# One more unit's w_out product by seven half-size products, its sums shared with VectorE, and the instruction list made anew

## The chip, the cores and the metric

The kernel runs on one core of a Trainium2 chip. Its engines are TensorE (PE, matrix products; PEld is its weight load), VectorE (DVE), ScalarE (ACT), GpSimd (POOL) and SyncE (SP, which issues the loads and stores); each works through a list of its own in order. The metric is the device time of one execution in microseconds (us).

## The reference

Packed attention, and a SwiGLU layer on its result, in fp32:

```python
p_packed = sm_attn(p, k, v)           # (8 batches, 8 heads, 32, 64), keys 576
out = sm_attn(q, p_packed, p_packed)  # (8, 8, 576, 64)
x = out.transpose(0, 2, 1, 3).reshape(4608, 512)
xn = x / sqrt(mean(x * x) + 1e-6) * rms_g
g, val = xn @ w_gate, xn @ w_val      # 512 to 1536
return (g * sigmoid(g) * val) @ w_out # 1536 to 512
```

## The kernel before

The 4608 tokens are worked in twelve units u = 0 to 11 of 384 tokens, three tiles of 128 each. For each unit the attention of its tokens comes first (the keys, the packed values and the weights of a batch are made once per batch), then the SwiGLU layer. Each fp16 product on TensorE stands for one of fp32: an operand is a hi and a lo half, and three products (hi by hi, hi by lo, lo by hi) are summed in PSUM.

*First product* (`mlp`, line 1527): for each of 12 slices ft of the 1536 columns, gate and val in a PSUM room each, six matmuls of 384 columns (twelve of 192 where the unit lies over two batches). `gated` takes them to SBUF: ScalarE's Silu (line 1609), VectorE's multiply (line 1612), then the hi half by ScalarE or VectorE and the lo half, a subtract, by GpSimd or VectorE (lines 1634, 1637, 1640), into the tile `hall`.

*Second product*: for one tile of tokens, 36 matmuls of 512 columns (12 slices by three, line 1592) into one PSUM room of four (pm), and a scaled copy to a tile of SBUF and a store (`store`, line 1800). For the units from `STR_FROM` = 6 on, only tile 2 is done so. Tiles 0 and 1 go by Strassen's method in Winograd's form (`seven`, line 1723): the two tiles and pairs of slices (a chunk c, six in all) form a 2 x 2 block matrix, w_out another, and seven products k = 1, 6, 7, 5, 2, 4, 3, each 18 matmuls of 256 columns, take the place of eight. What this needs:

- sums of blocks of the unit's gated tiles: `parts_of`, four adds or subtracts of 128x128 for each chunk (line 1677, by GpSimd or VectorE in turn, `SUM_BY`), cast to hi by ScalarE (line 1686) and to lo by GpSimd (line 1689); the halves of the blocks themselves by lines 1653, 1656 and 1659.
- sums of blocks of w_out, made once: `tees`, for each of six chunks (tee 0 to 5) two adds of 128x512 (line 1132) and four subtracts of 128x256 (line 1135), all by GpSimd (`TEE_BY`), then ScalarE's cast (line 1139) and VectorE's low (line 1141) into `teev`, a region of the tile wgv that is free once batch 3's packed weights are done.
- `together` (line 1738) adds the seven products up on VectorE and stores.

The order of the work is written out. Each part of the kernel is a generator (a chain); `Plan.run` goes through the table `ORDER`, at each entry lets the chain of that number issue its next step, and hands out rooms (PSUM and SBUF buffers) from pools as they are asked for. A step such as ("tee", d) waits until the mark is there. So the table fixes the order on every engine. `FILLS` puts dummy matmuls (line 1826) ahead of certain TensorE steps. Names of rooms in the rows: pm, psa and psb are PSUM; o_0x and o_1x are the two rooms that sums, tees and stores share; t and a are gated tiles.

Of the kernel before, what the change touches and what calls it, by code (L numbers as in the profile page):

```python
# [15 lines left out]
P = 128  # L16
# [28 lines left out]
class Plan:  # L45
# [84 lines left out]
    "ABAAAAAAAAAAADAAAWAEAFAAAAAAAAAAAAAAAAADAAAAAAAAAAAAABAxADAxAyADAxADAEAyAWAWAxAxAxAxAGAHAWAxAyAEAxAEAFAxAFAFAyAW"  # L130
    "AWAWAxAQAyAyAyAyAQAQAyAQAyACAGAyAQAIACAHAGAIAHACAQACAGACAIAJAXACARAHAXAXAIAXARAJACAJARAXAJAKARAKAXASASALAWALAWAX"
    "ARACAQAMAXAXASAKAYASALAKAXAXAXASAYALAXAXAzAXARATAWATAzAWAYATAXAXAMAXAzAMAXAYA0ATAMA0ATANAXANA0AOAPAaAAAAAAAAAzAA"
    "AAASAYANAbAYAUAcATANARAXA2A2AOAUA0AWAXA2AYAWAWAUA2AXAYAPA1AOASA3AOAUA3APAWAZAVAAAUAAAZAUAPA3A7A1AAAAAZAAA7AaAVAA"
    "AAAaA3AZAVAaATA8AAA1AbAAAAAbAYAAAVAaAAAaAbAAAAAZA8AcAcAVAcA8AYA9A9AZA5AdA7AdA8A7A-AdAeA-AdAbAZAZAcA9AZA+A-AeA+A5"
    "A9A-AZAZAZAfAeAcBAA5A+AeAdBAAVAfBAA+A6AfA1AbA6AYA5A4A4A5BAA5A5A5A6BBAeAZAZAeAdA5AfAUA6AfBCBBA1AVA6BCAZA6A6BCAfBB"
    "A6AgAYBBAgAZBEAgBEAZAZBDBDArA5BCBDA1BFA6A5ArA6AsBFBDBEAZACAZA6ACBEArACAsACAtACBGACBGAZAXACBFACAXBGAZAZAZBFAsBGAC"
    "ACBHACBIAWACACAZAXAtAYBHBIACAXAtAAAAAAAAAAAAAvBIAuAWAABHAZAZAZAZAZAZBHAZAZAuAXAWAAAXAAAZAZAXAuAZAvAXAYAXAXAZAWAA"
    "AwAYAZAZAwBJAXAvAABJAABJAXBJAZAZBIAXAwAXAXAWAZAZAZAZAAAXAXAWAXAXAWAWAWAZAZAZAZAZAZAXAWAXAZBKBLAWAAAXAYAAAAAXAABM"
    "AXBMAXAAAZBMAAAXAABMAZAZAZAXAABLBKAZAXAAAZAZAZAZAZAZAXAABNAZBOAZAXAYBOBPBPAYBOAZAXBPBOAABRAXBQBQAXBQAABQBRAZAZAZ"
# [45 lines left out]
    "EKAZAZAZAZEMAZAZAXAZAZAZAZAZAZEMEMEMAZAZELAZAZAZEMEMAZAZAZENEMAZENAZEMAZEMENEOAZAZEMEOEOAZEPAZENEPEQEQEPEOAZEOEO"
    "EQAZEOEOAZEPERESAZEOAZEREQEQEQEQEQEOESAZAZEQEOEOEQEREOETEOERETEQESEUESEQAZAZAZEUETESAZEUESEQESESESEVEVAZEUETEUES"
    "EWEWAZAZAZEUESEVEVEUEUEUEXEUAZEWEXEQEUEUEUEXEWEXAZAZAZEWEWEYEYEUEYEYEYEWESEYAZAZAZEWEYEWEWESEWEYEYEWESAZEYEWEYAZ"
    "AZAZEYAZEYEYAZEWAZAZAZAZAZEaAZAZAZAZAZEaAZEaAZEZEaEZAZAZAZAZAZAZEaEaEaEaAZEaAZEaEa"
# [1693 lines left out]
```

## Time and profile before

| | |
|---|---|
| time, median of 3 runs | 715.92 us (715.59 to 718.26) |
| the profiled execution | 717.6 us, its span 715.8 us, mean granted TensorE clock 0.998 |
| TensorE busy | 697.8 us, 97% of the span |
| VectorE, ScalarE, GpSimd busy | 515.4 us (72%), 496.2 us (69%), 350.1 us (49%) |
| chain that ended last | TensorE 81%, DMA 6%, VectorE 4%, ScalarE 4%, GpSimd 3% |

The span is shorter than the execution's time by what lies around it. A busy share is a mean over the whole span: an engine at 72% can be without a gap in one stretch and half idle in another. The chain is followed back from the last instruction, at each step to what released it. Line numbers are those of the kernel before; in the kernel after, lines from 190 on stand two lower in the file, those from `seven`'s wait on three.

### The profile page before, as it was taken

How to read it: one execution, taken by the hardware profiler on the slowest of the kernel's cores; microseconds unless marked ns; L12 is line 12 of the kernel's file. 1: busy time of each engine (PE TensorE's matmuls, PEld its weight loads, DVE VectorE, ACT ScalarE, POOL GpSimd, SP SyncE). 2: the span in 40 equal slices, each digit the busy share in tenths (PEclk: the TensorE clock that was granted, in tenths of full speed). 3: DMA queues.
4: the chain of work that ended last, by engine and by line, in shares of the span. 5: the costliest groups of instructions: out<-in, count | busy, mean ns of one | idle time of the engine just before them, and what ended most of it. 6: DMA issues, size and time to landing. Idle time of an engine off the chain costs nothing.

```text
span 715.8 us, 20438 instructions
## 1 busy us (share of the span) xinstructions
PE 697.8 (97%) x8367; PEld 460.4 (64%) x8367; DVE 515.4 (72%) x1126; ACT 496.2 (69%) x1095; POOL 350.1 (49%) x468
## 2 busy tenths in 40 slices
PE   8889999999999999989999999999999999999998
PEld 6755655874554564676454555886855766987656
DVE  4788898775976877767879988787666756665342
ACT  3588887886787787578687789588387466473350
POOL 2486632341343364456656459158158076165290
PEclk9999999999999999999999999999999999999999
DMA  9996903677288858964989769787747653421001
GB/s 294 367 375 260 239 3 83 104 164 167 50 166 186 253 136 209 210 115 145 247 225 210 183 113 248 162 224 234 186 138 192 124 164 64 148 104 38 31 0 45
DMA packets 157103, 118.23 MB, mean 165 GB/s; under 512 B 117201, under 2 KB 140497, under 8 KB 153170
## 3 DMA queue, kind: packets, MB, share of 16 engines
q1 hardware_dynamic: 157010, 116.94, 63.5%
q8 instruction: 65, 1.06, 0.6%
q14 instruction: 28, 0.23, 0.1%
HBM read 72.88 MB, written 15.73 MB: 124 GB/s over the span
## 4 chain that ended last, share of the span: by engine, by line
PE 81%; DMA 6%; DVE 4%; ACT 4%; POOL 3%; issue 2%; SPq 1%; POOLq 0%; ACTq 0%; DVEq 0%
PE pm_1x L1527 9%; PE pm_3x L1527 9%; PE pm_0x L1527 8%; PE pm_2x L1527 8%; PE pm_3x L1592 8%; PE pm_2x L1592 7%; PE pm_0x L1592 5%; PE pm_1x L1723 3%; PE pm_0x L1723 3%; PE pm_3x L1723 3%; PE pm_2x L1723 2%; DMA ring<-in_moe_w_gate_dram 2%; PE psa L1086 1%; PE psb L915 1%; PE psa L1327 1%
## 5 line engine op out<-in xcount | busy, mean ns | idle before, releaser
L1527 PEld LDWEIGHTS <-ring 128*128 128x128 f16 x2304 | 204.7, 98 | 86.5 <-issue 14.9
L1592 PEld LDWEIGHTS <-hall 128*128 128x128 f16 x792 | 74.9, 98 | 89.0 <-issue 4.0
L1656 POOL TENSOR_TENSOR hall<-a_0x,hall 128x384 f16<-128x384 f32 (+1 forms) x36 | 32.5, 903 | 64.9 <-ACT hall L1653 64.8
L1637 POOL TENSOR_TENSOR hall<-t_1x,hall 128x384 f16<-128x384 f32 x32 | 32.7, 1021 | 59.3 <-ACT hall L1634 52.0
L1592 PE MATMUL pm_2x<-wo,hall 128*128 128x512 f16 x252 | 57.3, 379 | 0.0
L1592 PE MATMUL pm_3x<-wo,hall 128*128 128x512 f16 x252 | 56.8, 379 | 0.0
L1592 PE MATMUL pm_0x<-wo,hall 128*128 128x512 f16 x216 | 48.3, 379 | 0.0
L1527 PE MATMUL pm_0x<-aTu_0x,ring 128*128 128x384 f16 (+1 forms) x318 | 45.8, 287 | 1.2 <-DVE t_1x L1612 0.8
L1527 PE MATMUL pm_1x<-aTu_1x,ring 128*128 128x192 f16 (+1 forms) x336 | 47.0, 283 | 0.0
L1723 PEld LDWEIGHTS <-hall 128*128 128x128 f16 x432 | 41.9, 98 | 5.9
L1527 PE MATMUL pm_3x<-aTu_1x,ring 128*128 128x384 f16 (+1 forms) x306 | 44.6, 288 | 0.1
L1527 PE MATMUL pm_1x<-aTu_0x,ring 128*128 128x384 f16 (+1 forms) x300 | 43.5, 288 | 0.3 <-DVE ring L373 0.2
L1159 POOL TENSOR_TENSOR wgv<-o_0x,wgv 128x512 f16<-128x512 f32 x19 | 22.9, 1203 | 34.9 <-ACT wgv L1157 34.9
L1527 PE MATMUL pm_3x<-aTu_0x,ring 128*128 128x192 f16 (+1 forms) x276 | 39.0, 284 | 0.4 <-ACT t_1x L1609 0.3
L1527 PE MATMUL pm_2x<-aTu_1x,ring 128*128 128x384 f16 (+1 forms) x258 | 37.7, 289 | 0.7 <-ACT t_1x L1609 0.7
L1527 PE MATMUL pm_2x<-aTu_0x,ring 128*128 128x384 f16 (+1 forms) x258 | 36.7, 285 | 0.3 <-ACT t_1x L1609 0.3
L1527 PE MATMUL pm_0x<-aTu_1x,ring 128*128 128x192 f16 (+1 forms) x252 | 35.5, 284 | 0.0
L1637 POOL TENSOR_TENSOR hall<-t_0x,hall 128x384 f16<-128x384 f32 x24 | 23.9, 997 | 19.7 <-ACT hall L1634 18.3
L884 POOL TENSOR_TENSOR a1T_0x<-a_1x 96x768 f32<-96x768 f16 x9 | 15.1, 1676 | 37.0 <-DMA a_1x<-hl_0x 25.4
L373 DVE SCALAR_TENSOR_TENSOR ring<-psa,ring 128x512 f16<-128x512 f32 x30 | 20.6, 686 | 11.5 <-ACT ring L371 11.5
L371 ACT ACTIVATE ring<-psa 128x512 f16<-128x512 f32 x30 | 17.8, 593 | 13.5 <-DVE ring L373 6.7
L1653 ACT CAST hall<-a_0x 128x384 f16<-128x384 f32 (+1 forms) x36 | 17.6, 488 | 9.0 <-DVE a_0x L1612 8.5
(1103 smaller groups left out, 1828.2 us busy)
## 6 DMA issues: line engine op xcount, KB each, us to landing
wgv<-wdram SPq DMA_DIRECT2D x24, 1024.0 KB, 6.0
wdram<-wgv SPq DMA_DIRECT2D x6, 1024.0 KB, 4.8
hall<-in_moe_w_out_dram SPq DMA_DIRECT2D x4, 1024.0 KB, 4.8
out_dram<-o_0x SPq DMA_DIRECT2D x14, 256.0 KB, 3.2
out_dram<-o_1x SPq DMA_DIRECT2D x13, 256.0 KB, 3.0
wo<-in_moe_w_gate_dram SPq DMA_DIRECT2D x3, 1024.0 KB
wo<-in_moe_w_val_dram SPq DMA_DIRECT2D x3, 1024.0 KB, 11.1
big_0x<-in_v_dram SPq DMA_DIRECT2D x4, 576.0 KB, 6.6
```

Source lines behind the costliest of these rows:

```text
L371: nc.scalar.activation(hi, x, AF.Copy, scale=s)
L373: nc.vector.scalar_tensor_tensor(lo, x, s, hi, ALU.mult, ALU.subtract)
L884: nc.gpsimd.tensor_tensor(a1T, x[:, 0], x[:, 1], ALU.add)
L915: nc.tensor.matmul(pp[32 * j : 32 * j + 32, :D], a1T[:, c, 32 * j : 32 * j + 32], vf[:, j, cv, :], start=(c == 0), stop=(c == NCK - 1),)
L1086: nc.tensor.matmul(ps[e][32 * j : 32 * j + 32, :], pg[h, lp, j, :], w16[h, j, lw, :], start=(n3 == 0), stop=(n3 == 2),)
L1159: nc.gpsimd.tensor_tensor(wgv16[:, c, k, 1], st, wgv16[:, c, k, 0], ALU.subtract)
L1527: nc.tensor.matmul(psi[:, :, o : o + n], pw[:, g, lw, w, f * P : (f + 1) * P], aT[:, :, la, g, o : o + n], start=(j == 0), stop=(j == 5),)
L1592: nc.tensor.matmul(po, hall[:, ft, lh, ts], wo[:, ft, 1 - lw, :], start=(n == 0), stop=(n == 3 * NFT - 1))
L1637: nc.gpsimd.tensor_tensor(hall[:, ft, 1, :], t, hall[:, ft, 0, :], ALU.subtract)
L1653: nc.scalar.copy(h3[:, 0, own], x3[:, own])
L1656: nc.gpsimd.tensor_tensor(h3[:, 1, own], x3[:, own], h3[:, 0, own], ALU.subtract)
L1723: nc.tensor.matmul(ps[:, :q], A[k](c, la), W[k](c, lw), start=(c + n3 == 0), stop=(c == NFC - 1 and n3 == 2))
```

## The change

Unit 5's second product is done by seven products too, and the rest follows: the sums of w_out must be there one unit sooner; tees 2 and 5 are made by VectorE; in unit 5 all sums of the gated tiles are VectorE's, in later units they stay shared. Products 1, 2 and 3, which use no tee, no longer wait for one. `ORDER` (3288 entries before, 3351 after) and `FILLS` (90 dummy matmuls before, 97 after) are made anew.

```diff
 ORDER = (
-    "ABAAAAAAAAAAAADAAAWAEAFAAAAAAAAAAAAAAAAADAAAAAAAAAAAAABAxADAxADAyADAxADAEAyAWAWAxAxAxAxAGAHAWAxAyAEAxAEAFAxAFAFAyAW"
...
+    "ABAAAAAAAAAADAAAAAAADAAAAAAAAAAAAAAAAAAAAAWADAAAAAAAEAFADABAGAHAxAyAxAWAyAxAWAxAEAxAxAxAWAxAyAWAFAEAEAxAxAyAFAyAy"
...
 FILLS = (
-    (0, 29, "pm", 0), (1, 4, "pm", 0), (8, 5, "pa", -1), (20, 3, "psc", 0), (23, 1, "psc", 0),
-    (24, 5, "psc", 0), (28, 37, "pm", 0), (31, 6, "pm", 0),
+    (0, 29, "pm", 0), (5, 4, "psc", 0), (12, 1, "pm", 0), (21, 2, "psc", 0), (24, 3, "psc", 0),
+    (26, 4, "pm", 0), (27, 2, "pm", 0), (28, 18, "pm", 0), (29, 15, "pm", 0), (31, 10, "pm", 0),
+    (42, 9, "psc", 0),
 )
...
-STR_FROM = 6
-TEE_BY = "PPPPPP"
+STR_FROM = 5
+TEE_BY = "PPDPPD"
...
-        by = nc.gpsimd if SUM_BY[c] == "P" else nc.vector
-        kind = (POOL, pool(P)) if SUM_BY[c] == "P" else (DVE2, dve(P))
+        by = nc.gpsimd if SUM_BY[c] == "P" and u > STR_FROM else nc.vector
+        kind = (POOL, pool(P)) if SUM_BY[c] == "P" and u > STR_FROM else (DVE2, dve(P))
...
-                        yield ("tee", d)
+                        if k > 3:
+                            yield ("tee", d)
```

TensorE, before, as unit 5's second tile ends and the third begins (psb is the attention's room, pm_1x and pm_3x those of two tiles):

```order
L948 MATMUL psb<-ident_66,pk_1x 128x128
L971 LDWEIGHTS margin
L971 MATMUL psb<-tiny_50x,margin 128x1
...
L1592 LDWEIGHTS hall
L1592 MATMUL pm_1x<-wo_78,hall 128x512
...
L1592 MATMUL pm_3x<-wo_78,hall 128x512
```

TensorE, after, at the same attention group, now within unit 5's tile 2, which comes first, with product 1 behind it:

```order
L950 MATMUL psb<-ident_66,pk_1x 128x128
L973 LDWEIGHTS margin
L973 MATMUL psb<-tiny_50x,margin 128x1
...
L1594 LDWEIGHTS hall
L1594 MATMUL pm_3x<-wo_78,hall 128x512
...
L1726 LDWEIGHTS hall
L1726 MATMUL pm_1x<-wo_78,hall 128x256
```

Where unit 5's tiles 0 and 1 had 72 matmuls of 512 columns there are seven products of 18 matmuls of 256; the attention groups between them stand earlier by some of unit 5's matmuls.

VectorE, before, around the scale usc_0x of the next unit; big, hl and ring are the attention's and the weights' lows:

```order
L1459 TENSOR_SCALAR trio_3x<-trio_2x,tiny_59x 128x3
L1141 TENSOR_TENSOR wgv<-o_0x,wgv 128x512
L373 SCALAR_TENSOR_TENSOR big_1x<-big_3x,tiny_66x,big_1x 128x512
L1468 TENSOR_SCALAR usc_0x<-gv_sc,tiny_58x 128x12
L373 SCALAR_TENSOR_TENSOR big_1x<-big_3x,tiny_66x,big_1x 128x512
L1800 TENSOR_SCALAR o_0x<-pm_0x,invE 128x512
```

VectorE, after, ahead of the same scale: the last chunks' sums (L1679, the former 1677) and the last low of tee 5 (L1143, the former 1141):

```order
L1679 TENSOR_TENSOR o_1x<-a_0x 128x128
L1679 TENSOR_TENSOR o_1x<-t_1x,o_1x 128x128
L375 SCALAR_TENSOR_TENSOR pd_0x<-pf_0x,tiny_65x,pd_0x 128x64
L626 COPY pd_0x<-pd_0x 128x4x64
L361 TENSOR_SCALAR uv_266<-psb 128x1
L365 TENSOR_SCALAR uv_266<-uv_266 128x1
L366 TENSOR_SCALAR tiny_71x<-uv_266 128x1
L1143 TENSOR_TENSOR wgv<-o_0x,wgv 128x512
L375 SCALAR_TENSOR_TENSOR ring<-psa,ring 128x512
L1461 TENSOR_SCALAR trio_3x<-trio_2x,tiny_63x 128x3
```

Before, unit 5 has no sums, and the tees go on behind this place. After, all 24 sums and all lows of the tees stand ahead of it, and so do the adds and subtracts of tees 2 and 5, which VectorE has from here:

```order
L1134 TENSOR_TENSOR o_1x<-wo_78 128x512
L1614 SCALAR_TENSOR_TENSOR t_1x<-pm_2x,usc_1x,t_1x 128x384
L1134 TENSOR_TENSOR o_0x<-wo_78 128x512
L1137 TENSOR_TENSOR o_1x<-o_1x 128x256
L1137 TENSOR_TENSOR o_1x<-o_0x,o_1x 128x256
```

These are tee 5's first five among unit 5's gated tiles; before, all adds and subtracts of tees are on GpSimd.

## Rows read from the trace of the kernel before

**Rows 1.** The page: busy time of the engines, and the chain by engine.
```profile
PE 697.8 (97%) x8367; PEld 460.4 (64%) x8367; DVE 515.4 (72%) x1126; ACT 496.2 (69%) x1095; POOL 350.1 (49%) x468
PE 81%; DMA 6%; DVE 4%; ACT 4%; POOL 3%; issue 2%; SPq 1%; POOLq 0%; ACTq 0%; DVEq 0%
```
**Rows 2.** Waits of TensorE, 0:100 and 100:715: total us, times, longest.
```profile
PE pm_3x L1074 <- DVE ring L373: 2.5, 2, 2.0
PE pm_1x L1826 <- POOL misc L276: 1.7, 1, 1.7
PE pm_0x L1527 <- DVE t_1x L1612: 0.8, 1, 0.8
PE pm_3x L1086 <- issue: 2.1, 1, 2.1
PE psb L915 <- DMA big_4x<-in_v_dram: 0.8, 1, 0.8
PE pm_2x L1527 <- ACT t_1x L1609: 0.7, 1, 0.7
```
**Rows 3.** Chain in order of time, 690:716: start us, us, what.
```profile
691.03 7.77 PE pm_2x L1592 x36
698.80 1.97 PE pm_3x L1723 x18
...
710.59 1.98 PE pm_2x L1723 x18
```
**Rows 4.** Windows of line 1826 alone: window, us, PE busy (x), PEld busy (x).
```profile
0.00:715.80 715.80, 12.88 (x90) 9.52 (x90) 1.00 0.64 165
```
**Rows 5.** Windows ahead of unit 5's second product: busy us and instructions per engine.
```profile
core 0: us, PE busy (x) PEld busy (x) DVE busy (x) ACT busy (x) POOL busy (x), PEclk, DMA share, GB/s
322.00:332.00 10.00, 10.00 (x134) 7.71 (x132) 6.11 (x19) 9.38 (x21) 8.14 (x10) 1.00 0.48 175
341.39:391.07 49.68, 49.68 (x540) 26.45 (x525) 42.14 (x80) 37.12 (x77) 31.89 (x32) 1.00 0.99 236
```
**Rows 6.** Waits of VectorE, 341.39:395.4: total us, times, longest.
```profile
DVE a_0x L1612 <- ACT a_0x L1609: 2.1, 3, 0.9
DVE ring L373 <- ACT ring L371: 1.6, 1, 1.6
```
**Rows 7.** Timeline of TensorE, 380:400: start us, us, what.
```profile
391.20 2.75 PE L1592 MATMUL pm_1x<-wo,hall 128*128 128x512 f16 x12
393.88 0.88 PE L915 MATMUL psb<-big_0x,a1T_0x 96*32 96x64 f32 x48
```
**Rows 8.** Line 1677, sums: ns min/median/max; its windows row, VectorE (x), GpSimd (x).
```profile
L1677 DVE TENSOR_TENSOR o_1x<-t_0x x5: 277/284/1000, 550.3 to 678.5; 128x128 f32<-128x128 f32 x5
...
0.00:715.80 715.80, 28.09 (x72) 34.23 (x72) 1.00 0.64 165
```
**Rows 9.** Lines 1141 and 1659, lows: by source, windows, and by form 341.39:391.07.
```profile
L1141 DVE TENSOR_TENSOR wgv<-wgv x5: 680/681/2314, 348.8 to 420.4; 128x512 f16<-128x512 f32 x5
0.00:715.80 715.80, 11.83 (x12) 1.00 0.64 165
L1659 DVE TENSOR_TENSOR hall<-t_1x,hall x8: 409/440/695, 416.2 to 680.2; 128x256 f16<-128x256 f32 x8
0.00:715.80 715.80, 3.96 (x8) 1.00 0.64 165
L1141 DVE TENSOR_TENSOR wgv<-wgv 128x512 f16<-128x512 f32 x3 | 3.7, 1225 | 0.0
```
**Rows 10.** Lines 1132 and 1135 on GpSimd: ns min/median/max, first and last start.
```profile
L1132 POOL TENSOR_TENSOR o_1x<-wo x5: 1155/1159/1797, 321.3 to 403.3; 128x512 f32<-128x512 f16 x5
L1135 POOL TENSOR_TENSOR o_1x<-o_1x x5: 727/728/1052, 326.2 to 406.2; 128x256 f32<-128x256 f32 x5
```
**Rows 11.** Windows of the head, columns as in rows 5.
```profile
0.00:20.00 20.00, 18.09 (x219) 13.24 (x219) 8.23 (x22) 7.15 (x12) 4.28 (x17) 1.00 0.95 290
20.00:40.00 20.00, 17.69 (x256) 15.57 (x260) 16.86 (x32) 11.27 (x21) 12.59 (x13) 0.91 1.06 377
```

More of the change, by code (lines that the diff above doesn't have):

```diff
@@ L135 @@
[L135 to L139, printed above, removed]
@@ L185 @@
[L185 to L188, printed above, removed]
+    "ABAAAAAAAAADAAAAAAADAAAAAAAAAAAAAAAAAAAAAWADAAAAAAAEAFADABAGAHAxAyAxAWAyAxAWAxAEAxAxAxAWAxAyAWAFAEAEAxAxAyAFAyAy"
@@ new lines @@
+    "AyAxAyAWAQAyAFAyACAQADAyAWAIAJACAGACACAHAGAHACAQACAQACACAGAQAIAKAXAIAHARAXAXARAIAXASARAXAJAQAKAJAJALARAQAKAXASAR"
+    "AXAYAXAWALAWALAXAXASAKALARAYAXASAzAXATAMANASATAzASAzAzATAXAXAYAMAWAXATAYAWA0AOATAMAYAXAXAXAMAYA0A0ATANA1AXA1A1AN"
+    "AXA0AYAWAUA2AWA1AXANAXAPAOAWAPARAOAUAXAaAAAAAAAAAUAAAAATAYA3AOAUAZAbAcA3APAVAWAAAUA2AAAZA7APA7ASAAAAAAAAAVAAAaAZ"
+    "A3AaAZAUAAAVAbAaAAA3AaAAAAA8AaAAAdAAAAAbAYAbA8AcAcAVAZAVAcA8AYA5A9A2AZA7A8AdA9A7AcA-AdA-AdAZAZAbAZA-A+A9AeAeA2Ac"
+    "A5A+A-AZA4AfBAA5AdAVAeA9BAAZAZA+AbBAA6AeA5AfBAAfA6A5A+A5A5AUAeA5A6AYAdAeBBAZAfAZA5BCAfA6BBBCA6AVA5AfA6BBAgAYA6AZ"
@@ new lines @@
+    "A2A5AgAgA4BCA6BDBCAZBBBEAZA6BDBEBDBDArA6ArAsA2A6AZACAZAsACBEAsACACACAZACACBFACAtArAZBFBEAXACACBGBGAZAZAZBFAXBFBG"
+    "AYBHACACBGACACAWAAAABIAZAAAXAtBIAWAZAuBHAZAZAAAZAZAAAAAXAtBIAvAAAWAuAZAZAZAAAXAXAuAwAXAvAAAAAWAAAZAXAYAXAXAZAWAZ"
+    "AXAAAZAZAZAZAWBHBJAwAYAXAXAXAvAWAAAWBHAZAZBJBJAwAWBIAZAZAZAXAWAZAZAXAZAXBJAXBLAWAXAXAXAAAXAAAYAZAZAAAAAAAZBKAZBM"
+    "AXAAAAAXAXAZAZBLBMAZAZBMAXAAAXAABMAXAZAZAZAZAZAZAZAXAABNAZAYBOAZAXBOBPBOAYBPAXAZAXBPBOBRBQBQAABPBQBQAAAXAABKAZAZ"
+    "BSBRAYAZAZBSBRAYBRAABTAABUBTAXAZAZBUBUBSBTBSAXAXBUBVAZAZBTAYBVAYAXAXBWBWAXAXBWBXAZAZBXBVBXAYBNBWAABYBYACBXBYACAY"
@@ new lines @@
+    "BaBaAXBaBYAZAZBbACBbAXBaBVAZACACAZBcACBbAZBbAXAZAZAXAXBcAZAWBZACAWBeAWAXAWAZAWBeAWBcAXACAXAXBeAZAZBcAZACAWACAXBd"
+    "AXBdAXACACAAAAAAAAAABdBdACAAACAZAABeACAZAZAZAXAAAAACAZAZAZAZAZAZAZAZAAACAWAZAZAZAAAWBZACAZAZAZACAAAZAZAZACAZBfAW"
+    "AAAAACAZAAACACAAAAACAZAZACACACACACACACACBgAZAAAYAZAZAWAAAXBfAYAAAZAZBhACAYAXAZAZBhAABhACBhAYAABiAXAZAZBkAABjAZAZ"
+    "AXAZBlBkBlAYBkBkBjBjAAAZAZBmAZBlBmBjAXBmBlBnAXBmAABnAYAZAZAYAYBgAhAABoBnBoBpAhBpBnAABqAAAZAZBpAhBpBqBrBqBqAXAZAZ"
+    "AAAXBsBrBoBrAZBsAZAZAXAhBrAhAXAXBsBuAXAYBuAhBuBoAZAZAZBsAhAXAXACBvAZBuBvAXAhBwBvACBwAZBvAhAXAhAYAhBxAZACAYBxACAC"
@@ new lines @@
+    "AXByACAYBwBwBzByAZBzAXBtAhAWAWBtBzBxByB0ACAhAXBzAZAZAZAXAZAZAZAZAXBxB0AZACAXAZAXAXAXAXBiB0AWAWACACACAhACACAAAAAh"
+    "B0AZACAWAZAZAZAZAZAZAZAZAZAZAAAXAZAZAZACAAACAAAWACAWACAAAhAZAWByB1AhACAhAZAZAWAWAWACAZAAAhAZACAhACACAAAhACAAAWAh"
+    "AAACAZAAACAAAhB1ACACAhACACB2ACAAAZACAZAZB2AZAXAhAAAYB3AXAZAZAZAhAAB3AXACB4AZAZAZB5B3AXAYAZAhB5AhB7B5B5AhB3AZAZB7"
+    "ACAXB8AhAhB7B8AZAZAXB7AZAZAhB6B6B6B9B8B6AhB9B8AAB9B9B-AhAhB-AhAhAAAZAZACAZAZB-B+B-AhAAAXAZCAACCAAACAAXAhCAAZAXAX"
+    "AAB+AAB+CBB+AZAXAZAACBAhAAB4AACBCCAXCCCBAZAZAZAZAXAhCCAXCCAXAXAXCDAhAXCECDAXAZAZCDAXCEAZAZAXAXCEAXAAAhAWAZAhCDCE"
```

89 lines of the change are left out of this document (39 added, 50 removed).

## The prediction

> **What bounds the kernel now.** I read the page's engine shares first, then TensorE's waits, then the end of the chain, and last the stretch in which the new work falls. TensorE is busy 97% of the span at full granted clock, and it holds 81% of the chain [rows 1]. So the kernel is as long as TensorE's work plus the few places where TensorE waits. Of these there are 2.1 us in the middle of the attention's matmuls, put down to nothing the profile shows ("issue"), 0.8 us for a load of v, and in the first 100 us pieces of 2.5, 1.7 and 0.8 us; at no second product of a unit is there a wait in the list [rows 2]. An edit can therefore help in two ways only: less TensorE work, or a wait less. It can hurt through any engine that comes late to a place where TensorE is now just served in time.
>
> VectorE is the one to watch. It is busy 72% of the span on average, but the average says little: I look at the stretch before unit 5's second product.
>
> **TensorE's saving.** In the last unit the chain shows both forms of a second product undisturbed: 36 matmuls of 512 columns for one tile take 7.77 us, and seven half-size products take 1.97, 1.97, 1.97, 1.97, 1.96, 1.97 and 1.98 us, 13.79 us together [rows 3]. Two tiles in the old form are 2 x 7.77 = 15.54 us. Unit 5 changes from the old form to the new, so TensorE's work falls by 15.54 - 13.79 = 1.75 us. The seven dummy matmuls more (97 for 90) cost at most 7 x 12.88 / 90 = 1.0 us [rows 4], but they stand where TensorE waits at the start; I take 0 for them.
>
> **What the new form asks of VectorE.** I take the stretch between two VectorE instructions that both lists have in the same sequence: the low half of a packed value (pav_2x<-pk_0x, 341.39 us) and the scale of the next unit (usc_0x<-gv_sc, 391.07 us). Before, VectorE has 79 instructions from the one to the other; after, it has 122. The other lines occur there as often as before, so the difference is 24 sums of 128x128 (four for each of the six chunks; in later units GpSimd keeps half of them), four adds of 128x512 and eight subtracts of 128x256 (the w_out sums of tees 2 and 5), two more lows of tees, and five short ones, for which two lows are narrower than before; I count these at nothing.
>
> In this stretch of 49.68 us VectorE was busy 42.14 us, so 7.54 us were free [rows 5]; they are waits for ScalarE and TensorE of at most 1.6 us each [rows 6], which a VectorE that runs late would swallow. From the end of the stretch to where TensorE would want the last of it there are about 4.3 us more: the first matmul group of L915 in unit 5's second product starts at 393.88 us, after 36 matmuls of the first tile and 12 of the next [rows 7]; in the new list the same group comes after 24 of unit 5's matmuls, not 48, so 24 x 0.216 = 5.2 us earlier, and from there to the third pair of chunks in product 6 lie 12 x 0.216 + 1.97 + 1.3 + 0.5 = 6.4 us, that is near 395.1 to 395.4 us. The row of the order with the last low of tee 5 stands five rows ahead of the stretch's end, so nearly nothing of the added work can be put off. The reserve is 7.54 + 4.3 = 11.8 us.
>
> The cost of the added work, from both sides:
> - 24 sums: the usual one takes 284 ns (median of a form), one beside GpSimd up to 1000; over all units the mean is 28.09 / 72 = 390 ns [rows 8]. So 6.7 to 9.4 us. I take 6.8: the sums of later units run beside GpSimd's own sums, which unit 5 has not.
> - 4 adds of 128x512, fp16 in: VectorE has no such row; the nearest is a tee's low of the same size, 680 ns undisturbed and 11.83 / 12 = 986 in the mean [rows 9]. From 2.7 to 3.9 us, and two more of those lows, 1.4 to 2.0; I take the middle, 5.0 together.
> - 8 subtracts of 128x256: again no row; the low of that size takes 409 to 695 ns, in the mean 3.96 / 8 = 495 [rows 9]. From 3.3 to 4.0 us; I take 3.8.
>
> Sum: 14.1 to 19.3 us, 15.6 taken. Against 11.8 us VectorE is late by 2.3 to 7.5 us, 3.8 taken. The stall lands on TensorE: behind the waiting weight load of product 6 its whole queue stands, the rest of unit 5's products and the attention groups between them. What TensorE loses there is not given back later.
>
> **What else moves, and its cover.** GpSimd gives up two of six tees but must end the other four by 395 us and not by 447 us. A pair of adds took 2 x 1.16 us and four subtracts 4 x 0.73 us undisturbed, 5.2 us a tee [rows 10]; in the stretch above GpSimd was busy 31.89 of 49.68 us [rows 5], so it has 17.8 us free. Its new work is 18 lows of the sums, of 128 or 256 columns; at the 0.73 us of a 256-column instruction [rows 10] that is 13 us at most. Hidden; without that cover it would join the same wait. ScalarE has 12.6 us free there for the 18 casts of the sums, 18 x 37.12 / 77 = 8.7 us at its mean instruction [rows 5]: hidden too. The tees' wait now stands only at the products that use them, so product 1 may start early; that takes no work away and costs nothing, as product 6 comes 1.97 us behind it.
>
> The head's list is new. The same loads stand in nearly the same sequence on SyncE's queue, and DMA is at 0.95 and 1.06 of its engines in the first two times 20 us [rows 11], so the order of the rest can hardly hurry it: 0, within 1 us either way. The other waits in the middle (2.1 + 0.8 + 0.7 and less) may each vanish or return elsewhere: 0, within 2 us. The tail is the same seven products and stores: 0.
>
> **The rule that bears on it.** In rows 8 and 9 the same VectorE instruction takes 284 or 1000 ns and 680 or 2314 ns, so something holds it at times. The Trainium skill, SBUF — State Buffer, section "SBUF: two separate sides", says that VectorE and GpSimd share one port pair as an exclusive lock, which a VectorE instruction with two SBUF inputs contends for against a GpSimd one that reads SBUF, and that the loser waits for the other's whole instruction. All added instructions are of this kind. The trace agrees in that both durations occur, but its mean of a sum, 390 ns, says that most go through unhindered. By my sum without such waits (14.1 us) the time would be 716.5 us; by the rule taken at its word, with every added instruction held, it would be above 720 us.
>
> **Sum.** -1.75 + 3.8 = +2.05 us. The profiled execution took 717.6 us with a span of 715.8, the three runs' median is 715.92, 1.7 us below; the change is put on the median, as both should shift alike: 718.0 us. From the bounds of this case, -1.75 + 2.3 - 1 to -1.75 + 7.5 + 1, it is 715.5 to 722.7 us.
>
> **Rivals.**
> 1. VectorE hides all of it. For it: VectorE had 3.9 of 10 us free in 322 to 332 us [rows 5], which would serve if it runs ahead, and the twelve w_out instructions need no unit's result. Against: the list puts none of the added instructions ahead of pav_2x, and the sums need unit 5's own gated tiles. Then only the saving is left: 715.92 - 1.75 = 714.2 us.
> 2. As 1, and the new list also loses the 2.1 us stall and the wait for v: 714.2 - 2.1 - 0.8 = 711.3 us. For it: the stall is tied to one place of the instruction stream, and that shifts. Against: the stream gets longer, and such a stall can come at another place.
> 3. Slower: every added instruction is held by a running GpSimd instruction. GpSimd is busy 31.89 / 49.68 = 64% of the stretch; half of a mean instruction of 31.89 / 32 = 1.0 us at 64% is 0.32 us for each of the 38. That is 12.2 us on top of 14.1, 26.3 in all; less 11.8 is 14.5 us late, and 715.92 - 1.75 + 14.5 = 728.7 us. It decides from the point where the added work exceeds the reserve by 5.3 us, that is, from 17.1 us or 0.08 us of such waiting for each of the 38. For it: three lows in the stretch took 1225 ns in the mean, not 680 [rows 9]. Against: the sums' own mean. A third of this hold (4 us) gives 720.5 us, where I put the case.
> 4. GpSimd's four tees are late instead. One tee more than its free time holds is 5.2 us: 719.4 us. Against: 17.8 us are free.
>
> **How the numbers follow.** The forecast, late by 2.3 to 5.3 us, has 0.40. Rival 1 has 0.24, rival 2 0.08, rival 3 0.24, rival 4 0.04. Half a per cent is 3.6 us, about what a measurement of this kernel can tell from no change: below 712.3 and above 719.5 us. Faster: most of rival 2, 0.07. Slower: rival 3, half of rival 4 and 0.05 from the forecast's own upper end, 0.31. The rest, 0.62, is no change. The likeliest case's own range is 715.5 to 719.5 us. For 8 in 10, rival 1 belongs in it with a margin, and rival 3 up to two thirds: 713.0 to 723.5 us.
>
> **What the profile after will show.** If I am right, TensorE has one or a few waits in unit 5's second product, 2 to 6 us together, put down to VectorE (a sum, a tee's low) or to a cast behind one; VectorE is busy without a gap for the 40 us ahead of it. If rival 1 holds, no such wait is in the list and TensorE's busy time falls by about 1.7 us with the span. If rival 3 holds, the sums and subtracts take over 500 ns in the mean in unit 5 and the wait exceeds 6 us. Rival 2 would show as a missing issue stall; rival 4 as a wait whose chain ends in GpSimd's adds or subtracts. A gain or loss ahead of 300 us of more than 1 us would make my reading of the head wrong.

## The result, and the profile after

The kernel after takes 728.04 us in the median of three runs (726.75 to 730.04), before 715.92; the ratio is 1.0145 with a 95% interval of [1.0113, 1.0178], as all ratios here. It is slower by 12 us. The forecast was 718.0 us, within 713.0 to 723.5, so it was wrong by 10 us. Measured once more beside other kernels the ratio was 1.0163 [1.0132, 1.0194]. The profiled execution took 726.75 us with a span of 724.8; its 9.0 us more than the span before are what the rows below can explain; the other 3 us of the 12 lie in which execution was profiled (before above its median, after below).

The page of the kernel after, busy time and chain, as in [rows 1]:

```profile
PE 698.6 (96%) x8428; PEld 465.9 (64%) x8428; DVE 532.6 (73%) x1167; ACT 500.5 (69%) x1116; POOL 342.9 (47%) x474
PE 69%; DVE 10%; ACT 8%; DMA 7%; issue 3%; SPq 1%; POOL 1%; ACTq 0%; DVEq 0%; POOLq 0%
```

TensorE is busy 0.8 us longer and idle 26.2 us in place of 18.0. The chain has gone over to VectorE, ScalarE and DMA for a quarter of the span. The waits of TensorE after 100 us (total us, times, longest) answer to the last three of [rows 2]:

```profile
PE psb L917 <- POOL a1T_0x L886: 2.8, 2, 1.4
PE pm_0x L1529 <- issue: 1.5, 1, 1.5
PE psb L917 <- DMA big_3x<-in_v_dram: 1.2, 1, 1.2
PE pm_0x L1529 <- ACT t_1x L1611: 1.2, 1, 1.2
PE pm_3x L1594 <- ACT t_1x L1611: 0.8, 1, 0.8
PE pm_0x L1088 <- ACT t_1x L1611: 0.7, 1, 0.7
PE pm_1x L1529 <- issue: 0.7, 1, 0.7
PE pm_2x L1529 <- DVE ring L375: 0.7, 1, 0.7
```

No wait is above 1.5 us, and none stands at the half-size products, line 1726 here. Two stand in unit 5's second product, ahead of and within its tile 2, 0.78 us for ScalarE's Silu and 1.32 us for GpSimd's copy. TensorE's timeline (start, us, in brackets the wait) shows them, and unit 5's products 1.96 us apart; the second is product 6, which the forecast had waiting for a tee:

```profile
391.67 5.34 PE L1594 MATMUL pm_3x<-wo,hall 128*128 128x512 f16 x24 [0.78 <-ACT t_1x L1611]
...
398.33 0.88 PE L917 MATMUL psb<-big_5x,a1T_0x 96*32 96x64 f32 x48 [1.32 <-POOL a1T_0x L886]
...
402.01 2.13 PE L1726 MATMUL pm_1x<-wo,hall 128*128 128x256 f16 x18
403.97 2.13 PE L1726 MATMUL pm_2x<-wgv 128*128 128x256 f16 x18
405.94 2.13 PE L1726 MATMUL pm_0x<-wgv,hall 128*128 128x256 f16 x18
```

So the time went in small pieces. To see where, I divided each trace at the first multiply of `gated` of every unit (the 1st, 13th, 25th ... instruction of line 1612 on VectorE) and took span less TensorE's busy time from the windows between. TensorE's idle us in each stretch, by the units whose first multiply bounds it:

| kernel | to 1 | 1-2 | 2-3 | 3-4 | 4-5 | 5-6 | 6-7 | 7 to end | sum |
|---|---|---|---|---|---|---|---|---|---|
| before | 10.1 | 0.7 | 0.2 | 0.6 | 2.1 | 0.0 | 0.1 | 4.2 | 18.0 |
| after | 9.7 | 2.3 | 0.5 | 2.9 | 1.8 | 3.7 | 1.3 | 4.1 | 26.2 |
| after, a second execution (c1) | 9.9 | 2.1 | 0.5 | 2.6 | 1.6 | 4.1 | 1.3 | 4.1 | 26.2 |
| new list, unit 5 in the old form (a2) | 9.8 | 2.4 | 0.5 | 2.7 | 1.7 | 2.2 | 2.4 | 4.1 | 25.7 |
| new list to unit 4 only (h2) | 11.2 | 2.4 | 0.5 | 3.3 | 2.2 | 0.0 | 0.1 | 4.3 | 23.9 |
| after, added work cut to 16 columns (x7) | 9.9 | 2.5 | 0.5 | 3.0 | 2.6 | 2.3 | 1.4 | 4.1 | 26.2 |

(The rows come from the profiled execution of each; sums are of the unrounded values.) The two executions of the kernel after differ by at most 0.4 us in a stretch. Half of the growth, 4.1 of 8.2 us, lies between units 1 and 4, ahead of any work that the change adds: the first add of a tee starts at 323.6 us. The busy time per line closes the account: the second products take 16.07 us less in the old form and 14.27 us more in the new (-1.80 us), the dummy matmuls 14.79 us for 12.88 (+1.91), the first product 294.89 for 293.91 (+0.98), the rest -0.3; with 8.2 us of idle time that is 9.0 us.

### The profile page after: what moved, and what is told of

Read it like the earlier page. It is cut to its first block, busy times and chain, and to the rows that moved or that the text cites. A ratio compares the mean times of both kernels' runs of the same rounds, so it can differ in the third digit from the quotient of the medians.

```text
span 724.8 us, 20631 instructions
## 1 busy us (share of the span) xinstructions
PE 698.6 (96%) x8428; PEld 465.9 (64%) x8428; DVE 532.6 (73%) x1167; ACT 500.5 (69%) x1116; POOL 342.9 (47%) x474
## 4 chain that ended last, share of the span: by engine, by line
PE 69%; DVE 10%; ACT 8%; DMA 7%; issue 3%; SPq 1%; POOL 1%; ACTq 0%; DVEq 0%; POOLq 0%
PE pm_3x L1529 7%; PE pm_0x L1529 7%; PE pm_2x L1594 7%; PE pm_1x L1529 7%; PE pm_2x L1529 6%; PE pm_3x L1594 4%; PE pm_0x L1726 4%; PE pm_1x L1726 4%; PE pm_2x L1726 3%; PE pm_1x L1594 3%; PE pm_0x L1594 3%; PE pm_3x L1726 3%; DMA wo<-in_moe_w_gate_dram 2%; DMA a_1x<-hl_0x 2%; ACT ring L373 1%
## 5 line engine op out<-in xcount | busy, mean ns | idle before, releaser
L1639 POOL TENSOR_TENSOR hall<-t_1x,hall 128x384 f16<-128x384 f32 x28 | 28.0, 1000 | 61.9 <-ACT hall L1636 53.8
L1594 PE MATMUL pm_3x<-wo,hall 128*128 128x512 f16 x216 | 48.1, 379 | 0.8 <-ACT t_1x L1611 0.8
L1529 PE MATMUL pm_3x<-aTu_0x,ring 128*128 128x384 f16 (+1 forms) x300 | 43.5, 288 | 1.8 <-ACT pts_0x L964 1.4
L1529 PE MATMUL pm_2x<-aTu_0x,ring 128*128 128x192 f16 (+1 forms) x312 | 43.5, 283 | 0.3 <-ACT t_1x L1611 0.3
L1529 PE MATMUL pm_0x<-aTu_1x,ring 128*128 128x192 f16 (+1 forms) x306 | 43.5, 285 | 0.0
L1529 PE MATMUL pm_3x<-aTu_1x,ring 128*128 128x192 f16 (+1 forms) x306 | 43.5, 285 | 0.0
L1529 PE MATMUL pm_1x<-aTu_1x,ring 128*128 128x384 f16 (+1 forms) x282 | 40.2, 285 | 1.5 <-issue 0.7
L1658 POOL TENSOR_TENSOR hall<-t_0x,hall 128x384 f16<-128x384 f32 x20 | 20.5, 1027 | 34.2 <-ACT hall L1655 34.2
L1529 PE MATMUL pm_1x<-aTu_0x,ring 128*128 128x192 f16 (+1 forms) x240 | 33.2, 282 | 0.7 <-ACT a1T_0x L869 0.7
L1594 PE MATMUL pm_1x<-wo,hall 128*128 128x512 f16 x144 | 32.4, 379 | 0.2
L1639 POOL TENSOR_TENSOR hall<-t_0x,hall 128x384 f16<-128x384 f32 x22 | 22.2, 1008 | 14.9 <-ACT hall L1636 8.5
L373 ACT ACTIVATE ring<-psa 128x512 f16<-128x512 f32 x30 | 17.8, 594 | 14.2 <-DVE ring L375 9.0
## 6 DMA issues: line engine op xcount, KB each, us to landing
wo<-in_moe_w_gate_dram SPq DMA_DIRECT2D x3, 1024.0 KB, 15.6
```

The lines of the kernel that those rows point to most:

```text
L373: nc.scalar.activation(hi, x, AF.Copy, scale=s)
L1529: nc.tensor.matmul(psi[:, :, o : o + n], pw[:, g, lw, w, f * P : (f + 1) * P], aT[:, :, la, g, o : o + n], start=(j == 0), stop=(j == 5),)
L1594: nc.tensor.matmul(po, hall[:, ft, lh, ts], wo[:, ft, 1 - lw, :], start=(n == 0), stop=(n == 3 * NFT - 1))
L1639: nc.gpsimd.tensor_tensor(hall[:, ft, 1, :], t, hall[:, ft, 0, :], ALU.subtract)
L1658: nc.gpsimd.tensor_tensor(h3[:, 1, own], x3[:, own], h3[:, 0, own], ALU.subtract)
```

## The experiments

The theories as they stand in the expectations: (1) VectorE has too much to do ahead of unit 5's second product; (2) the list made anew is itself worse, whatever unit 5 does; (3) GpSimd is late with the tees or its copies, or holds VectorE; (4) the new list sets consumers too close behind what feeds them; (5) as 2, and it loses a little in every unit; (6) it loses at one place. Lists were mixed so that every part keeps its own sequence: the entries up to a point come from one list, the remaining ones from the other in its order.

**The list from end to end, and in halves.** a1 is the new `ORDER` and `FILLS` without the change:

```diff
-STR_FROM = 5
-TEE_BY = "PPDPPD"
+STR_FROM = 6
+TEE_BY = "PPPPPP"
 ORDER = ( the new list; unit 5's steps of the products in the old form at their places
...
```

> The new list from start to end, with unit 5's second product in the old form (36 matmuls of 512 columns for each tile, no sums in unit 5) and all tees on GpSimd at the list's new places. Theory 1 (VectorE has too much to do ahead of unit 5's second product): with 24 sums and 12 w_out instructions off VectorE most of the loss goes, 716 to 719 us. Theory 2 (the new list is itself worse, whatever unit 5 does): 722 to 728 us.

Measured: 738.87 us, ratio 1.0304 [1.0268, 1.0340]. Slower than the kernel after, against both theories, since this edit brings a cost of its own: all six tees on GpSimd at places made for four. The longest wait of TensorE ahead of unit 6 is GpSimd's there:

```profile
PE pm_3x L1593 <- POOL hall L1638: 4.7, 1, 4.7
PE psb L916 <- POOL a1T_0x L885: 1.9, 2, 1.0
```

That called for the same again with tees 2 and 5 on VectorE (a2):

```diff
-STR_FROM = 5
+STR_FROM = 6
 TEE_BY = "PPDPPD"
 ORDER = ( as in a1
...
```

> The new list with unit 5's second product in the old form and no sums in unit 5, but tees 2 and 5 on VectorE as in the kernel after, so that GpSimd isn't the engine that comes late as in the first run. Theory 4: the list's own cost without the change's 24 sums, 6 to 9 us above the kernel before, 0.8 to 1.3% slower; the saving of 1.8 us is missing here. Theory 1: 1 to 3 us above, up to 0.4% slower.

Measured: 730.48 us, ratio 1.0173 [1.0142, 1.0204]. This is the run that decides. Without the 24 sums, without a half-size product in unit 5, the new list is as slow as the kernel after. It keeps two things of the change, the tees a unit sooner and two of them on VectorE; what these cost it doesn't tell. Its waits are the same ones at nearly the same times:

```profile
PE psb L916 <- POOL a1T_0x L885: 3.4, 3, 1.5
PE pm_1x L1528 <- ACT t_0x L1610: 2.1, 2, 1.5
PE pm_0x L1528 <- issue: 1.4, 1, 1.4
PE psb L916 <- DMA big_3x<-in_v_dram: 1.3, 1, 1.3
```

The two halves, h2 with the new list up to unit 4's first product and the old kernel behind it, h1 the reverse:

```diff
 ORDER = ( h2: the new list's entries up to step 240 of the two products, then the old list's remaining ones
 ORDER = ( h1: the old list's entries up to step 240, then the new list's remaining ones
...
```

> The reverse: the new list and the new dummy matmuls up to unit 4's first product, from there the old list, with unit 5's second product in the old form. Theory 1: 716 to 719 us. Theory 2: 721 to 727 us. The two halves' losses should add up to some 12 us with the run before.

Measured: 724.24 us, ratio 1.0086 [1.0055, 1.0118].

> The old list and the old dummy matmuls up to unit 4's first product (near 300 us), from there the new list, with the change to unit 5. TensorE's idle time grew by 3.2 us between 100 and 300 us and by 5.0 us between 335 and 460 us. Theory 1 (the stretch before unit 5's second product): 720 to 724 us, as the second part stays. Theory 2 (the new list's start): 714 to 718 us, as only the saving is left.

Measured: 726.56 us, ratio 1.0114 [1.0083, 1.0146]. Each half is slower on its own. h2 is theory 2's case, and there nothing of the change runs at all, so its 6 us are the order's (with its dummy matmuls). h1 lies above either forecast: its TensorE is idle 5.3 us longer from unit 5 to unit 7 and busy 3.3 us longer over the span, at a granted clock of 0.992. By their medians the halves lose 15 us together, not the 12 expected. Finer cuts, h3 (the new list up to unit 2) and h5 (the old list up to unit 5):

> The new list and new dummy matmuls up to unit 2's first product (near 188 us), then the old list, unit 5's second product in the old form. Theory 5 (the new list loses a little in every unit that it orders anew, in waits on chains through ScalarE, VectorE, DMA and GpSimd, whatever unit 5 does): the unit 1 to unit 2 stretch alone, some 3 us, 0.2 to 0.6% slower than the kernel before. Theory 6 (one place between units 2 and 4 makes the 6 to 8 us of the run with the new list to unit 4): 0 to 0.2% slower.

Measured: 720.68 us, ratio 1.0040 [1.0018, 1.0061]. So a little over one unit of the new list costs some 3 us, as theory 5 had it, and the rest of the 6 us of h2 comes after it.

> The old list and old dummy matmuls up to unit 5's first product (near 354 us), then the new list with the change. Theory 5: only units 5 and 6 are ordered anew; they took 3.6 and 3.7 us more in the kernel after than before, of which the saving of 1.8 us is taken off already, so 0.6 to 1.1% slower than the kernel before. Theory 1 (the change's own work): 1% or more, as the old list has left more of the tees for after unit 5's start.

Measured: 727.30 us, ratio 1.0136 [1.0106, 1.0166], above theory 5's range in the middle and inside theory 1's. The first wait of unit 5 is 2.9 us for ScalarE's Silu, which the kernel after does not have; that the old list's start has not prepared what the new list's unit 5 expects is my reading of it. A seam may cost too, and h1 and h5 do not tell the change from it.

**The change without the new list.** x4 keeps the old list and sets unit 5's own instructions and the tees at the steps which the new list gives them; x6 shares the sums with GpSimd besides:

```diff
-STR_FROM = 6
-TEE_BY = "PPPPPP"
+STR_FROM = 5
+TEE_BY = "PPDPPD"
 ORDER = ( the old list; tees, and unit 5's gated tiles and stores, by the new list's steps
...
```

> The old list and the old dummy matmuls throughout; only the instructions of the change itself (unit 5's gated tiles, sums, products and stores, and the tees) stand at the places, counted in TensorE's steps of the two products, that the new list gives them. Theory 1 (unit 5 asks too much of VectorE): the stretch of unit 5 loses as in the kernel after, which from 324 to 475 us fell back by 3.8 us more, the saving already taken off, so 4 us above the kernel before, 0.4 to 0.9% slower. Theory 2 (the list made anew is what costs): 1.8 us faster to no change.

Measured: 751.49 us, ratio 1.0444 [1.0410, 1.0477], far outside both. TensorE's longest waits are for the attention's copy (a1T), a Silu and a hi half (pgh):

```profile
PE psb L916 <- POOL a1T_0x L885: 6.9, 1, 6.9
PE pm_0x L1528 <- ACT a_0x L1610: 3.9, 1, 3.9
PE pm_1x L1087 <- ACT pgh_0x L372: 3.3, 1, 3.3
```

> As x4, with 12 of unit 5's 24 sums on GpSimd. Theory 1: 2 to 4 us below x4. Theory 3: 1 to 4 us above it, as the kernel after rose by 1.8 to 2.6 us in the same edit.

Measured: 749.58 us, ratio 1.0429 [1.0395, 1.0464], no different from x4. The run shows that the change can't be put into the old list in this way; it doesn't show what a list with care for both would give.

**The added work.** e3 gives GpSimd half of unit 5's sums:

```diff
-        by = nc.gpsimd if SUM_BY[c] == "P" and u > STR_FROM else nc.vector
+        by = nc.gpsimd if SUM_BY[c] == "P" else nc.vector
```

> The kernel after, but in unit 5 GpSimd makes half of the sums (12 of 24), as in later units. Theory 1: VectorE has 12 x 0.28 to 0.39 = 3.4 to 4.7 us less ahead of the second product, so 723 to 726 us. Theory 2: no change, 727 to 729 us, or some us more if GpSimd is late with the tees.

Measured: 730.68 us, ratio 1.0182 [1.0149, 1.0215]: no gain, theory 1's 723 to 726 us is missed. x3 makes the sums and tees that VectorE took over small and leaves their places and waits, x5 does so with GpSimd's tees, x7 with both:

```diff
+            if u == STR_FROM:
+                d, a, b = d[:, :16], a[:, :16], b[:, :16]
             by.tensor_tensor(d, a, b, op)
...
+            n = 16 if TEE_BY[i] == "D" else 512     # x5: "P"; x7: every tee
-            by.tensor_tensor(x, wo[:, f, 1, :], wo[:, f, 0, :], ALU.add)
+            by.tensor_tensor(x[:, :n], wo[:, f, 1, :n], wo[:, f, 0, :n], ALU.add)
...
```

> The kernel after, but the 24 sums of unit 5 and the 12 adds and subtracts of tees 2 and 5 work on 16 columns only, so the outputs from unit 5 on are not the reference's. Their places, waits and count stay. That takes some 24 x 0.3 + 4 x 0.7 + 8 x 0.4 = 13 us less 36 x 0.1 = 9 to 10 us off VectorE. Theory 1: unit 5's part of the loss goes, 4 to 6 us below the kernel after, 722 to 724 us. Theory 2: within 1 us of it, 727 to 729 us.

Measured: 727.81 us, ratio 1.0120 [1.0090, 1.0151].

> The kernel after, but the adds and subtracts of the four tees on GpSimd work on 16 columns only (outputs from unit 5 on are not the reference's). That takes 4 x 5.2 = 21 us less some 4 x 6 x 0.25 = 15 us off GpSimd, and with it what GpSimd holds VectorE up. Theory 1 as it stands (VectorE's own work): 0 to 2 us below the kernel after, 726 to 728 us. Theory 3 (GpSimd is late with the tees and its copies for the attention, or holds VectorE): 3 to 6 us below, 722 to 725 us.

Measured: 727.41 us, ratio 1.0121 [1.0084, 1.0158].

> The kernel after with all 24 sums of unit 5 and the adds and subtracts of all six tees on 16 columns (outputs from unit 5 on are not the reference's): some 10 us off VectorE and 15 us off GpSimd at once. Theories 1 and 3 together: 4 to 6 us below the kernel after, 722 to 724 us. Theory 4: 1 to 2 us below, 726 to 727 us, as either alone gave.

Measured: 726.97 us, ratio 1.0124 [1.0098, 1.0151]. The three agree, 0.2 to 0.4% under the two measurements of the kernel after: 2 to 3 us at most, and the intervals overlap. x3 lies in theory 2's range, x5 in that of theory 1 as it stands, x7 in theory 4's; none comes near the 722 to 725 us that were expected of a VectorE or GpSimd with too much to do. The windows of 345 to 400 us (columns as in [rows 5]) show what was taken away, first in the kernel after, then in x7:

```profile
345.00:400.00 55.00, 51.27 (x564) 27.20 (x563) 51.27 (x109) 39.51 (x90) 34.60 (x41) 1.00 1.04 224
```

```profile
345.00:400.00 55.00, 52.71 (x579) 27.38 (x561) 44.08 (x103) 41.44 (x93) 21.25 (x37) 1.00 1.02 231
```

VectorE falls from 51.27 to 44.08 us of 55 and GpSimd from 34.60 to 21.25, and TensorE's idle time between units 5 and 6 falls by 1.4 us (by the table); over the whole span it stays at 26.2 us. Of the waits of 350 to 440 us, 4.9 us in the kernel after, 3.3 us stay, with VectorE at 80% and GpSimd at 39%. The longest are:

```profile
PE pm_3x L1596 <- ACT t_1x L1613: 1.3, 1, 1.3
PE pm_0x L1531 <- ACT t_1x L1613: 1.2, 1, 1.2
PE pm_3x L1088 <- DVE t_0x L1616: 0.4, 1, 0.4
```

**Two repairs.** The wait of 1.44 us at 175.5 us in the kernel after stands at the end of this chain (start, us, what):

```profile
163.18 3.71 DMA aTu_0x<-hl_0x
...
166.97 0.69 ACT hl_0x L373
...
167.69 0.76 DVE hl_0x L375
...
168.47 5.21 DMA a_1x<-hl_0x
...
173.84 1.64 POOL a1T_0x L886
```

One tile hl_0x serves two transposes one after the other; the second can't be filled before the first has left. Before, the same copy began at 170.66 us and its matmul started 0.7 us after the copy's end:

```profile
170.66 1.64 POOL L884 TENSOR_TENSOR a1T_0x<-a_1x 96x768 f32<-96x768 f16 x1 [7.91 <-DMA a_1x<-hl_0x]
173.03 0.88 PE L915 MATMUL psb<-big_0x,a1T_0x 96*32 96x64 f32 x48
```

Now TensorE waits for it. p1 was to put the three steps that waited for such copies or for v two steps later:

```diff
 ORDER = ( the new list; the attention's steps of L917 at product steps 170, 256 and 318 behind the next two
...
```

> The kernel after, with three steps of the attention (the matmuls of L917, which wait for a transpose by DMA, a copy by GpSimd or a load of v: 1.44, 1.24 and 1.32 us) put behind the next two steps of the two products each, and what follows in the same chain with them. Theory 4 (the new list sets consumers too close behind the DMAs, table loads and copies that feed them; no engine is over its limit): the three waits go, 3 to 4 us below the kernel after, 724 to 726 us. Theory 1 and 3 (VectorE or GpSimd full): the waits come back at the next step, 727 to 729 us.

Measured: 731.75 us, ratio 1.0196 [1.0167, 1.0225]. The edit moved other steps than its expectation says. In the kernel after, the matmuls of L917 that wait begin at 175.52, 298.96 and 398.33 us; those that p1 moved, by 12 matmuls or fewer each, began at 235.61, 322.67 and 382.77 us and waited for nothing. The first wait it aimed at stands where it was (kernel after, then p1):

```profile
175.52 0.88 PE L917 MATMUL psb<-big_1x,a1T_0x 96*32 96x64 f32 x48 [1.44 <-POOL a1T_0x L886]
```

```profile
175.53 0.88 PE L917 MATMUL psb<-big_1x,a1T_0x 96*32 96x64 f32 x48 [1.38 <-POOL a1T_0x L886]
```

So p1 doesn't test theory 4. What it shows is that three steps without a wait, put two steps later, made the kernel no faster: TensorE is idle 2.0 us longer than in the kernel after. The second repair is on ScalarE, whose timeline before TensorE's wait of 1.21 us at 430 us is:

```profile
425.29 0.57 ACT L1611 ACTIVATE a_0x<-pm_3x,usc_0x 128x384 f32<-128x384 f32 x1
425.88 1.28 ACT L1348 ACT_TABLE_LOAD   x1
427.17 0.94 ACT L1348 ACTIVATE e_0x<-e_0x,tiny_76x 128x768 f32<-128x768 f32 x1
428.13 1.28 ACT L1611 ACT_TABLE_LOAD   x1
429.42 0.58 ACT L1611 ACTIVATE t_1x<-pm_0x,usc_0x 128x384 f32<-128x384 f32 x1
```

An exponential between two Silus costs two loads of 1.28 us; TensorE waits for the second Silu to free a room. The new list has 34 such loads where the old has 32. p2 joins the exponentials as the old list has them:

```diff
 ORDER = ( the new list; the attention's exponential ahead of unit 6's first Silu, one of the packed values behind unit 5's last
...
```

> The kernel after, with one exponential of the attention moved ahead of unit 6's first Silu and one of the packed values behind unit 5's last, so that ScalarE goes from Silu to exponential and back as often as in the kernel before (two table loads of 1.28 us fewer). Theory 4: TensorE's wait of 1.21 us at 430 us goes and perhaps half of the 0.78 us at 391 us, 1 to 2 us below the kernel after, 726 to 727 us. Theory 1: no change, 727.5 to 728.5 us.

Measured: 732.66 us, ratio 1.0205 [1.0176, 1.0233]. Two loads fewer, and slower. The wait of 0.78 us at 391 us went, but 1.5 us for an exponential and 2.3 us for a copy stand near it, and in place of the 1.21 us at 430 us there are 1.6 us at 427, for another Silu. Theory 4 fails in this one place, where a chain moved to save a load brought longer waits in its neighbours; for the three waits that p1 aimed at it is untested.

**The dummy matmuls.** b1 is the kernel before with the new `FILLS` alone:

> The kernel before with the new table of dummy matmuls (97 for 90, at other steps) and nothing else. The kernel before ran at a mean granted clock of 0.993 to 0.998, the kernel after at 0.998 to 1.0. If the new places alone keep the clock up, it rises to 0.999 or 1.0 and the time falls by 1 to 3 us; if the clock hangs on the list around them, time and clock stay within 0.2%.

Measured: 724.46 us, ratio 1.0089 [1.0058, 1.0120]. The forecast had the sign wrong. TensorE's windows show why (first b1, then before; busy us first, granted clock third from the end):

```profile
28.00:34.00 6.00, 3.54 (x41) 2.94 (x38) 5.72 (x8) 3.39 (x4) 4.55 (x7) 1.00 1.05 387
34.00:40.00 6.00, 5.34 (x41) 4.63 (x42) 3.11 (x8) 2.90 (x3) 4.79 (x7) 0.72 1.07 359
```

```profile
28.00:34.00 6.00, 6.00 (x50) 5.53 (x50) 5.47 (x7) 3.29 (x4) 4.76 (x7) 0.72 1.06 388
34.00:40.00 6.00, 6.00 (x120) 5.35 (x122) 5.84 (x12) 3.56 (x6) 5.59 (x6) 1.00 1.06 359
```

In the kernel before the clock falls once, near 28 us, and the 37 dummy matmuls of one step stand over a wait for VectorE. With 18 there TensorE stands idle (3.13 us, up to 34.66 us), the clock falls behind it, and the next step has 15 dummy matmuls, about half of them at the fallen clock. The matmul behind them starts at 38.42 us, before at 36.01:

```profile
35.97 2.62 PE L1827 MATMUL pm_0x<-misc,margin 128*128 128x256 bf16 x15
38.42 0.17 PE L473 MATMUL pm_1x<-tiny_13x,margin 128*128 128x2 bf16 x1
```

```profile
36.01 0.17 PE L472 MATMUL pm_1x<-tiny_13x,margin 128*128 128x2 bf16 x1
```

A second fall follows (0.88 in 46 to 60 us, where before has 1.00). The dummy matmuls of b1 answer to [rows 4]:

```profile
0.00:719.00 719.00, 16.57 (x97) 11.13 (x97) 1.00 0.64 164
```

They take 3.7 us more than before. TensorE's idle time is 17.8 us for 18.0 and its busy time 701.2 for 697.8, so in this execution the dummy matmuls make up the 3.2 us that the span is longer. The median is 7 us above; in the seven runs of b1 the mean granted clock was 0.987 to 0.995, and how the rest divides is not shown. So the tables belong together, and that the kernel after holds 0.998 to 1.0 while the kernel before lies at 0.988 to 1.0 is the new list with its fills, not the fills alone. This gain of the clock, an estimate of up to some 0.3% of the time from the mean clocks, is inside the 1.45% already.

> The kernel after, beside the same runs of the kernel before as the other three, so that the differences between them have one base: 1.1 to 1.8% slower, as measured first.

Measured: 729.62 us, ratio 1.0163 [1.0132, 1.0194], as expected.

## Why the prediction was wrong, by its steps

*TensorE's saving, 1.75 us.* Right: 1.80 us by the busy times of the two lines. In time it is too small to be seen by itself; a2, which lacks it, is slower than the kernel after by 0.1 to 0.3%, with overlapping intervals.

*VectorE's added work, 14.1 to 19.3 us, 15.6 taken.* Right in size. The windows of 335 to 400 us, of single lines of the kernel after (sums, adds, subtracts; VectorE's busy us and count, then GpSimd's) answer to [rows 8, 9]; 18 of the 24 sums lie in them:

```profile
335.00:400.00 65.00, 6.23 (x18) 0.00 (x0) 1.00 0.92 198
335.00:400.00 65.00, 2.95 (x4) 10.05 (x6) 1.00 0.92 198
335.00:400.00 65.00, 4.18 (x8) 9.72 (x12) 1.00 0.92 198
```

A sum (line 1679) took 6.23 / 18 = 346 ns, an add of 128x512 (line 1134) 738 and a subtract of 128x256 (line 1137) 523, so 24 x 0.346 + 2.95 + 4.18 and two lows at 0.71, the mean of the ten there, are 16.9 us.

*VectorE late by 3.8 us, on product 6.* This did not happen. No product waited; the 2.1 us of wait in unit 5's second product are put down to ScalarE and GpSimd. What x7 takes away of the work, with GpSimd's, is worth 0.2 to 0.4%, or 1.4 us of TensorE's idle time in unit 5, spread over waits for Silus, tiles and copies ahead of the products. The row that comes nearest is that of the tees' lows on VectorE (ns min/median/max, first and last start):

```profile
L1143 DVE TENSOR_TENSOR wgv<-o_0x,wgv x6: 675/722/1116, 339.1 to 403.7; 128x512 f16<-128x512 f32 x6
```

The last one began at 403.73 us and took 1.12, up to 404.85. Product 6, begun at 403.97, uses it first in its 17th matmul, 16 x 0.109 = 1.7 us later, so it was there with 0.9 us to spare; in the second execution (c1) with 0.1. It was close. TensorE came to this place some 10 us later than the prediction had it: in the kernel after it has been idle 7.1 us longer by then, and the dummy matmuls took 1.9 us more. That was VectorE's reserve. Whether VectorE would have been late had TensorE lost nothing before was not tried; in h5, where TensorE lost 4.7 us up to there and product 6 began 1.0 us sooner, none of the products waited either, with 0.1 us to spare.

*The rest of the list, "0, within 1 us" for the head and "0, within 2 us" for the middle.* This is the step that failed. The head to unit 1 was even (128.8 us against 129.0). The middle was not: 4.1 us more of idle time from unit 1 to unit 4, where h2, without any of the change, has 4.6, and 4.9 us more from unit 5 to unit 7, where a2, without the sums and half-size products, has 4.5. The term was put at 0; it measured 8.2 us of idle time in all. The prediction's own sign of this, a loss of more than 1 us ahead of 300 us, was there: 3.0 us more of idle time up to 300 us. I had looked at the old list's waits, found 4 us of them, and taken that as a measure of how much a new order could move. But a wait that the old list doesn't show can be near. In the nine groups of matmuls that use GpSimd's copy a1T from 150 to 450 us, the old list has the matmul 0.05 to 2.3 us behind the copy's end. The 0.7 us of the copy at 170.66 us became the wait of 1.44 us, and 0.2 us at 393.88 us the one of 1.32. That the rest of the loss comes about in the same way, in some 280 chains, is my reading; it was not measured.

*The dummy matmuls, 0.* They took 1.91 us more of TensorE's time, above the 1.0 us given as the most. The clock's gain in the two profiled executions, 0.998 to 1.0, is of that size (an estimate: 0.002 x 716 = 1.4 us), and the head came out even, so the 0 was right by luck.

*The rivals.* The third gave 728.7 us, near the measured 728.0, for a reason that is not there. It needed 12.2 us of waiting for GpSimd on top of 14.1 us of added work; the added work took 16.9, which leaves 2.8. Sums took 346 ns where it had 600; the subtracts' mean, 523 ns, is above its sign of 500, but by two of eight (646 and 1016 ns beside a GpSimd low; the others 410 to 426). And x5, which takes GpSimd's tees nearly away, gains no more than x3. Of the Trainium skill's rule (SBUF — State Buffer, "SBUF: two separate sides") this trace shows such single cases, and not the price on every instruction. That the new list by itself is slower, with the change a small gain on top, was among no rival: by the medians the kernel after is 1 to 2 us faster than a2, which the intervals don't tell from nothing.

*What stays open.* Why each wait of the new list arose, and whether a list could be found in which unit 5's new form pays its 1.8 us. x4, x6 and p2 show only that three simple ways don't lead there, and p1 tried another edit than was meant. a2's list was made for a unit 5 with the sums and early tees, so how much of the loss from unit 5 on a list made for the old form would have is open too. Nor is the 0.98 us that the first product's matmuls are longer explained.

## What to carry to other kernels

Where a change comes with an order made anew, the order is a change of its own, and here it was the larger one: forecast it apart, with a range that allows for slacks that the old order's waits don't show. (How wide such a range should be was not measured.) The first experiment is then the new order without the change; here it was as slow as the kernel after. VectorE at 9 tenths in a stretch cost little, as TensorE met its results late enough, and taking its work away showed how little in one run. And an edit that moves steps is to be looked up in the trace of the run: p1 moved steps that had no wait.

## What the runs showed of the hardware

- ScalarE loads a table on a change between Silu and exponential: 1283 ns each, 32 in the kernel before and 34 after. The Trainium skill, ScalarE: Activation LUTs, "What ACT_TABLE_LOAD costs", gives the same 1283 ns and about 1380 ns of drain besides. The load agrees; of the drain this trace shows nothing: the load at 425.88 us begins 0.02 us after the Silu before it ended and the exponential 0.01 us after the load.
- TensorE's granted clock fell to its lower level (1.2 of 2.4 GHz) for a few us behind idle time near the start: in b1 behind a wait of 3.13 us (0.72 in 34 to 40 us), where a dummy matmul of 256 columns took 422 ns and otherwise 272, and again behind a wait of 2.03 us (0.88 in 46 to 60). In the kernel before the same wait of 2.03 us had no fall behind it. The executions of one kernel differ in it: of 18 of the kernel before, those at a mean of 0.990 took 718.99 to 720.41 us, those at 0.998 714.84 to 718.07.
- A transpose by DMA of a 128x1536 fp16 tile took 5.2 us (a_1x<-hl_0x) in the kernel after, another 3.7 us (aTu_0x<-hl_0x), and the next write of the source, hl_0x, began 0.08 us after the latter's end.
